# Block-sparse attention and a gated feed-forward on one core: k and q loaded in token chunks, full-width turns, scores and AV products of two pairs side by side, a split last step

## The chip, the cores and the metric

The kernel runs on one core of a Trainium2 chip. The metric is the device time of one execution in microseconds. One more execution is recorded by the hardware profiler, and all rows below come from that one. Engines are named as the profile names them: PE is TensorE's matmuls, PEld its weight loads, DVE is VectorE, ACT is ScalarE, POOL is GpSimd and SP is SyncE.

## The reference, cut to what matters

```python
batch, n_heads, seq, head_dim = 4, 8, 768, 64          # block 32, window 16
k_sum = k.reshape(B, H, nb, block, D).max(axis=3)       # 24 blocks
v_sum = v.reshape(B, H, nb, block, D).mean(axis=3)
scores_l = scale * q @ k.T            # kept where |i - j| < window
scores_s = scale * q @ k_sum.T + log(block)
a = softmax(concat([scores_l_masked, scores_s]))
x = (a @ concat([v, v_sum])).transpose(0, 2, 1, 3).reshape(3072, 512)
ffn = (gelu(x @ w_gate) * (x @ w_val)) @ w_out          # 512 -> 1536 -> 512
out = x + sigmoid(x @ w_res) * ffn
```

Inputs are float32; the matmul operands are bfloat16, and GpSimd's DMAs convert on the way in.

## The kernel before, in words

**Units.** The 3072 tokens are cut into eight units of 384, two halves of each of the four batches; unit u is half u % 2 of batch u // 2. The eight heads are four pairs hp of 128 rows (two heads of 64). The schedule is written out by hand: each engine runs its instructions in the order in which the program issues them.

**Loads and turns.** k and q come from memory with tokens on partitions. For batches 1 to 3 `load_batch` (L162) issues, on GpSimd's queue, one transfer for all of k, one for all of q (96 partitions, each with eight tokens in one run of 2 KB per head, L87), and seven for v (L96: chunks of 128 tokens with all heads, runs of 256 B). It is called within unit 0 for batch 1, and at the start of units 1 and 3 for batches 2 and 3. A turn (`turn_pair`, L169) brings one pair to d on partitions: 16 PE transposes of 96 tokens by 64 (L174), the two heads to the two halves of the partitions. ScalarE copies the result out, to `kW` (`k_step`, L178, where VectorE then adds the window's neighbours and the block maxima) or to `qT` (`q_step`, L193). In units 1, 3 and 5 each of the first eight of twelve steps `fo` turns one k or one q of the next batch.

**A unit's gate and value part.** For each of twelve `fo` there are four matmuls `g` and four `vv` (L300, 384 tokens wide), a gelu on ScalarE (L306) and a product on VectorE into `gvT` (L307). The pool `ps_mm` has four PSUM banks; `g`, `vv`, `r` and `f` take the bank that came free first.

**Block means.** `vsum_sum` (L198) takes the means of v over blocks on TensorE (`vs`, L204): seven matmuls with 32 weight columns, into partitions 96 to 127. It stands once in the start and once each in units 1, 2 and 4.

**A unit's tail.** After the twelve steps the unit's own output and the next unit's attention run in one written order (L475 to L503). For its own output there are, for each of three `sub` of 128 tokens: `r` and a tanh (`res_step`, L326), twelve `f` (`ffn_step`, L329), and `end_step` (L337: two VectorE operations `th` and `o`, and the output DMA on SyncE). For the next unit there are, for each pair: `s_step` (L234: twelve `s` matmuls of 64 rows by 64 columns, an exponential on ScalarE, a mask on VectorE giving `P`), `av_step` (L280: twelve `ao` matmuls and the normalising on VectorE, `rz` and `xn`), `xt_step` (L284: three transposes `xp` and a copy to `xT` on VectorE). There is one PSUM home each for `s` (two banks), `ao` and `xp`. So the order on TensorE is s0, r0, f0, ao0, s1, r1, four f1, ao1, s2, eight f1, ao2, s3, xp0, r2, four f2, ao3, xp1, eight f2, xp2, xp3, and then the next unit's first `g`. Unit 0 has an order of its own (L446 to L472), and in unit 7 only the output part remains.

Of the kernel before, what the change touches and what calls it, by code (L numbers as in the profile page):

```python
# [8 lines left out]
F32 = mybir.dt.float32  # L9
# [6 lines left out]
def kernel(  # L16
# [22 lines left out]
    QT = 64  # L39
# [29 lines left out]
    bmean = const.tile([128, NB - 2 + 32], BF16, name="bmean")  # L69
# [30 lines left out]
    with tc.manual_schedule():  # L100
# [42 lines left out]
        select(bmean[:], ALU.is_ge, 0.0, 32 * (NB - 2) - WIN, -32, 1)  # L143
        select(bmean[:], ALU.is_ge, 0.0, 31 + WIN - 32 * (NB - 2), 32, -1)
# [17 lines left out]
        def load_batch(b):  # L162
            k_sb[b], q_sb[b] = token_tile(0, S, "k_sb"), token_tile(0, S, "q_sb")
# [5 lines left out]
        def turn_pair(src, hp, pool, tag):  # L169
            pj = src.shape[2]  # L170
# [5 lines left out]
            return tp  # L176

        def k_step(b, hp, pool, tag):  # L178
            tp = turn_pair(k_sb[b], hp, pool, tag)
            kw = kW[b % 2][hp]  # L180
            nc.scalar.copy(kw[:, :, OWN:OWN + QT].rearrange("d t (p j) -> d t p j", j=8),  # L181
                           tp.rearrange("d j (t p) -> d t p j", t=NT))
# [10 lines left out]
        def q_step(src, b, lo, hi, hp, pool, tag):  # L193
            tp = turn_pair(src, hp, pool, tag)
            nc.scalar.copy(qT[b % 2][hp][:, lo:hi].rearrange("d (p j) -> d p j", p=PP),  # L195
                           tp.rearrange("d j p -> d p j"))

        def vsum_sum(b, pool, tag, chunks=range(NC + 1), vs=None):  # L198
            if vs is None:
                vs = pool.tile([128, DM], F32, tag=tag, name="vs")  # L200
            for c in chunks:
                lo = NB - 2 - 4 * c if c < NC else 0
                rows, t = (slice(0, 128), 2 * c) if c < NC else (slice(64, 64 + WIN), NT - 1)
                nc.tensor.matmul(vs[96:128, :], bmean[rows, lo:lo + 32], vext[b % 2][rows, t, :, 0:D],  # L204
# [29 lines left out]
        def s_step(u, hp, st, s=None):  # L234
            b, half = u // 2, u % 2
            first = s is not None
            if not first:
                s = ps_s.tile([128, 2, 512], F32, tag="s", name="s")
            kw, qt = kW[b % 2][hp], qT[b % 2][hp]
            for t in range(HT):  # L240
                tt = half * HT + t
                for hh in range(2):
                    ps = slice(hh * 64, hh * 64 + 64)
                    nc.tensor.matmul(s[:, hh, t * QT:(t + 1) * QT], kw[ps, tt, :],  # L244
# [3 lines left out]
            nc.scalar.activation(P.rearrange("p a t q -> p a (t q)"), s[:, :, 0:TU], AF.Exp,  # L248
                                 scale=scale, bias=bias_t[:])
            if not first:  # L250
                Pf = P.rearrange("p a t q -> p (a t) q")
                nc.vector.tensor_mul(Pf, Pf, maskt.unsqueeze(1).to_broadcast([128, 2 * HT, QT]))  # L252
            st["P", hp] = P

# [74 lines left out]
        def ffn_step(st, gvT, sub, lo, hi):  # L329
# [3 lines left out]
            for fo in range(lo, hi):  # L333
                nc.tensor.matmul(st["f", sub][:], gvT[:, fo, ss], w_out[:, fo, :],  # L334
                                 start=(fo == 0), stop=(fo == FO - 1))

        def end_step(u, st, sub):  # L337
            f, th = st["f", sub], st["th", sub]
            nc.vector.scalar_tensor_tensor(th[:], th[:], 1.0, f[:], ALU.add, ALU.mult)  # L339
            o = work.tile([128, DM], F32, tag="o", name="o")  # L340
            nc.vector.scalar_tensor_tensor(o[:], th[:], 0.5, st["xn"][:, sub, :], ALU.mult, ALU.add)  # L341
            row = u * TU + sub * 128
            nc.sync.dma_start(out=out[row:row + 128, :], in_=o[:])
# [72 lines left out]
        for u in range(NU):  # L416
# [29 lines left out]
            if u == 0:  # L446
# [12 lines left out]
                av_step(n, 1, nst)  # L459
# [5 lines left out]
                av_step(n, 3, nst)  # L465
# [9 lines left out]
            if nst:  # L475
                s_step(n, 0, nst)
            res_step(st, 0)
            ffn_step(st, gvT, 0, 0, FO)
            if nst:
                av_step(n, 0, nst)  # L480
                s_step(n, 1, nst)
            end_step(u, st, 0)
            res_step(st, 1)
            ffn_step(st, gvT, 1, 0, 4)
            if nst:
                av_step(n, 1, nst)
                s_step(n, 2, nst)
            ffn_step(st, gvT, 1, 4, FO)
            if nst:
                av_step(n, 2, nst)  # L490
                s_step(n, 3, nst)
                xt_step(n, 0, nst, *TT)
            end_step(u, st, 1)
            res_step(st, 2)
            ffn_step(st, gvT, 2, 0, 4)
            if nst:
# [38 lines left out]
```

## Time and profile before

| | us |
|---|---|
| runs of the kernel before | 285.95, 286.34, 287.6 |
| their median | 286.34 |
| the profiled execution's own time | 285.99 |
| its span, first to last instruction | 284.3 |
| granted TensorE clock, share of full speed | 1.00 |

The span is the part that the rows of the profile show; 1.7 us of the profiled execution's time lie around it. A row of a timeline gives the start and the duration in us, the engine, the line, the operation, the array's rows*columns for TensorE, what is written and read, and how many instructions were merged. A row of a group gives the number of instructions, then busy us and the mean ns of one, then the idle time of the engine just before them and what ended it. A row of waits gives us in total, how many, and the longest. A row of a DMA issue gives its size and the us from issue to landing. Matmuls are pipelined, so a matmul's duration overlaps the next one's.

### The profile page before, as it was taken

The page shows a single profiled execution, that of the slowest core. Times are in us where ns is not written, and L with a number is a line of the kernel's source. Part 1 is how long each engine was busy: PE and PEld are TensorE (multiplying, and loading weights), DVE is VectorE, ACT ScalarE, POOL GpSimd, SP SyncE. Part 2 cuts the span into 40 slices and gives each one's busy share as a digit, 9 for nine tenths or more (in the row PEclk, how much of TensorE's full clock was granted, in tenths as well). Part 3 has the DMA queues.
Part 4 walks back from the last instruction along what each step waited for, and adds up shares of the span by engine and source line. Part 5 has one row for each costly group of instructions (what it writes and reads, how often), then busy time and mean ns, then how long its engine had stood idle before and what let it go on. Part 6 is the DMA issues. An engine that isn't in the chain of part 4 may idle for free.

```text
span 284.3 us, 6276 instructions
## 1 busy us (share of the span) xinstructions
PE 270.6 (95%) x2607; PEld 147.5 (52%) x2632; DVE 173.2 (61%) x429; ACT 138.4 (49%) x214; POOL 44.7 (16%) x65
## 2 busy tenths in 40 slices
PE   7789997999999999999999999999999999999993
PEld 2445553555445555555555555455555555455541
DVE  3675826685557963785538855686536963683422
ACT  2855377066464335546566235446654445444310
POOL 8975532461103000040000000000000000000000
PEclk9999999999999999999999999999999999999999
DMA  6999999999952900190001100101001100101001
GB/s 89 167 179 197 201 205 208 158 241 175 171 97 55 111 0 0 39 115 19 2 0 40 76 0 1 39 37 39 2 1 39 74 2 0 39 37 39 0 37 74
DMA packets 44043, 21.36 MB, mean 75 GB/s; under 512 B 25840, under 2 KB 40944, under 8 KB 44016
## 3 DMA queue, kind: packets, MB, share of 16 engines
q0 software_dynamic: 40560, 14.68, 51.8%
q1 hardware_dynamic: 3456, 6.29, 6.0%
q8 instruction: 20, 0.33, 0.5%
q14 instruction: 7, 0.06, 0.1%
HBM read 29.36 MB, written 6.29 MB: 125 GB/s over the span
## 4 chain that ended last, share of the span: by engine, by line
PE 89%; POOL 3%; DMA 3%; issue 1%; DVE 1%; ACT 1%; POOLq 0%; DVEq 0%
PE g L300 23%; PE vv L300 22%; PE f L334 21%; PE r L318 8%; PE tp L174 4%; PE ao L268 4%; PE s L244 3%; DMA vext<-in_v_dram 3%; PE xp L287 2%; PE vs L204 2%; POOL vext L96 1%; ACT P L248 1%; PE gv L300 1%; POOL k_sb L87 1%; DVE xn L278 0%
## 5 line engine op out<-in xcount | busy, mean ns | idle before, releaser
L306 ACT ACTIVATE ge<-g 128x384 f32<-128x384 f32 x95 | 46.7, 491 | 71.0 <-DVE gvT L307 36.5
L300 PE MATMUL g<-xT,w_gate 128*128 128x384 bf16 x380 | 79.3, 327 | 0.0
L307 DVE TENSOR_TENSOR gvT<-ge,vv 128x384 bf16<-128x384 f32 x95 | 52.3, 552 | 42.9 <-PE vv L300 41.7
L300 PE MATMUL vv<-xT,w_val 128*128 128x384 bf16 x380 | 77.7, 326 | 0.0
L334 PE MATMUL f<-w_out,gvT 128*128 128x512 bf16 x274 | 65.9, 379 | 1.4 <-issue 1.1
L300 PEld LDWEIGHTS <-w_val 128*128 128x128 bf16 x384 | 37.5, 98 | 26.3 <-issue 1.9
L300 PEld LDWEIGHTS <-w_gate 128*128 128x128 bf16 x384 | 35.0, 98 | 23.5 <-issue 2.0
L248 ACT ACTIVATE P<-s,bias_t 128x768 bf16<-128x768 f32 x32 | 28.9, 902 | 28.1 <-PE s L244 28.0
L334 PEld LDWEIGHTS <-gvT 128*128 128x128 bf16 x288 | 26.9, 98 | 29.8
L96 POOL DMA_DIRECT2D vext<-in_v_dram x28 | 23.0, 830 | 63.2 <-PE ao L268 46.9
L252 DVE TENSOR_TENSOR P<-P,maskt 128x768 bf16<-128x768 bf16 x28 | 15.6, 556 | 18.0 <-ACT P L248 18.0
L318 PE MATMUL r<-w_res,xT 128*128 128x512 bf16 x88 | 24.0, 381 | 0.4
L339 DVE SCALAR_TENSOR_TENSOR th<-th,f 128x512 f32<-128x512 f32 x24 | 16.3, 681 | 8.9 <-PE f L334 8.9
L181 ACT COPY kW<-tp 128x768 bf16<-128x768 bf16 x16 | 12.8, 799 | 12.2 <-PE tp L174 12.2
L278 DVE TENSOR_TENSOR xn<-ao,rz 128x384 bf16<-128x384 f32 x32 | 17.8, 557 | 1.1
L324 ACT ACTIVATE th<-r 128x512 f32<-128x512 f32 x24 | 14.3, 594 | 8.5 <-PE r L318 8.1
L195 ACT COPY qT<-tp 128x768 bf16<-128x768 bf16 (+1 forms) x20 | 13.3, 673 | 8.9 <-PE tp L174 8.8
L341 DVE SCALAR_TENSOR_TENSOR o<-th,xn 128x512 f32<-128x512 f32 x24 | 16.6, 692 | 0.8
L268 PEld LDWEIGHTS <-P 128*64 128x64 bf16 (+2 forms) x432 | 9.5, 110 | 13.4 <-DVE P L252 5.5
L276 DVE RECIPROCAL rz<-ao 128x6 f32<-128x6 f32 x32 | 6.1, 191 | 13.6 <-PE ao L268 13.6
L268 PE MATMUL ao<-vext,P 128*64 128x65 bf16 (+1 forms) x384 | 11.8, 199 | 1.5 <-DVE xn L278 1.5
L318 PEld LDWEIGHTS <-xT 128*128 128x128 bf16 x96 | 8.1, 98 | 7.4
(66 smaller groups left out, 198.0 us busy)
## 6 DMA issues: line engine op xcount, KB each, us to landing
out_dram<-o SPq DMA_DIRECT2D x24, 256.0 KB, 2.0
vext<-in_v_dram POOLq DMA_DIRECT2D x20, 128.0 KB, 10.5
k_sb<-in_k_dram POOLq DMA_DIRECT2D x3, 768.0 KB, 11.1
q_sb<-in_q_dram POOLq DMA_DIRECT2D x3, 768.0 KB, 14.3
w_gate<-in_moe_w_gate_dram POOLq DMA_DIRECT2D x6, 256.0 KB, 8.6
w_val<-in_moe_w_val_dram POOLq DMA_DIRECT2D x6, 256.0 KB, 8.7
w_out<-in_moe_w_out_dram POOLq DMA_DIRECT2D x3, 512.0 KB, 14.1
k_sb<-in_k_dram POOLq DMA_DIRECT2D x2, 384.0 KB, 5.9
```

The source lines that it names most:

```text
L96: nc.gpsimd.dma_start(out=dst, in_=v[b, :, lo:hi, :].rearrange("h p d -> p h d"))
L248: nc.scalar.activation(P.rearrange("p a t q -> p a (t q)"), s[:, :, 0:TU], AF.Exp, scale=scale, bias=bias_t[:])
L252: nc.vector.tensor_mul(Pf, Pf, maskt.unsqueeze(1).to_broadcast([128, 2 * HT, QT]))
L268: nc.tensor.matmul(ao[64 * e:64 * e + 64, sub, hh, :], P[rows, hh, t, :], rhs, start=blocks is None or (not blocks and sub == 0 and hh == ...
L278: nc.vector.tensor_mul(xn, ao[:, :, :, 0:D], rz.to_broadcast([128, NSUB, 2, D]))
L300: nc.tensor.matmul(acc[:, 0:TU], w[:, ko, fs], st["xT"][:, ko, :], start=(ko == 0), stop=(ko == KO - 1))
L306: nc.scalar.activation(ge[:], g[:, 0:TU], AF.Gelu)
L307: nc.vector.tensor_mul(gvT[:, fo, :], ge[:], vv[:, 0:TU])
L318: nc.tensor.matmul(r[:], st["xT"][:, ko, ss], w_res[:, ko, :], start=(ko == 0), stop=(ko == KO - 1))
L334: nc.tensor.matmul(st["f", sub][:], gvT[:, fo, ss], w_out[:, fo, :], start=(fo == 0), stop=(fo == FO - 1))
L339: nc.vector.scalar_tensor_tensor(th[:], th[:], 1.0, f[:], ALU.add, ALU.mult)
L341: nc.vector.scalar_tensor_tensor(o[:], th[:], 0.5, st["xn"][:, sub, :], ALU.mult, ALU.add)
```

## The change

1. `load_batch` loads k and q of batches 1 to 3 in six chunks of 128 tokens each, with all heads in a partition's row, in runs of 256 B: 12 transfers for a batch in place of two.
2. `turn_pair` turns these by six full 128x128 transposes, one for a chunk, instead of sixteen.
3. `vsum_sum` uses 128 weight columns instead of 32, and `bmean` grows from 54 to 150 columns.
4. In the tails of units 1 to 6, s0 and s1 stand together, ao0, ao1, s2 and s3, and ao2 and ao3. s1 and s3 write two single banks, one for each head, with one exponential for each. The mask of pair 3 is issued behind `end_step` of sub 0. The `xT` copies move from VectorE to ScalarE, and each of ao and xp uses both single homes in turn.
5. In unit 0's tail ao1 and ao3 use a bank of `ps_mm`.
6. In unit 7 the last sub's `f`, `th`, `o` and output DMA are done in two halves of 256 columns.

```diff
-    bmean = const.tile([128, NB - 2 + 32], BF16, name="bmean")
+    bmean = const.tile([128, NB - 2 + 128], BF16, name="bmean")
...
-            load_tokens(k_sb[b], k, b, 0, S, 0, H)
-            load_tokens(q_sb[b], q, b, 0, S, 0, H)
+            for sb, src, name in ((k_sb, k, "k_sb"), (q_sb, q, "q_sb")):
+                sb[b] = qk.tile([128, NC, H, D], BF16, tag=name, name=name)
+                for c in range(NC):
+                    nc.gpsimd.dma_start(out=sb[b][:, c],
+                                        in_=src[b, :, c * 128:(c + 1) * 128, :].rearrange("h p d -> p h d"))
...
+            if src.shape[1] == NC:
+                tp = pool.tile([128, S], BF16, tag=tag, name="tp")
+                for c in range(NC):
+                    nc.tensor.transpose(tp[:, c * 128:(c + 1) * 128],
+                                        src[:, c, 2 * hp:2 * hp + 2, :].rearrange("p h d -> p (h d)"), ident[:])
...
-                nc.tensor.matmul(vs[96:128, :], bmean[rows, lo:lo + 32], vext[b % 2][rows, t, :, 0:D],
+                nc.tensor.matmul(vs[:], bmean[rows, lo:lo + 128], vext[b % 2][rows, t, :, 0:D],
...
-        def s_step(u, hp, st, s=None):
+        def s_step(u, hp, st, s=None, two=None, masked=True):
...
+            if two:
+                s = [pool.tile([128, 512], F32, tag=tag, name="s1") for pool, tag in two]
...
+            if two:
+                for hh in range(2):
+                    nc.scalar.activation(P[:, hh].rearrange("p t q -> p (t q)"), s[hh][:, 0:TU], AF.Exp,
+                                         scale=scale, bias=bias_t[:])
...
-                av_step(n, 1, nst)
+                av_step(n, 1, nst, *MM)
...
-                av_step(n, 3, nst)
+                av_step(n, 3, nst, *MM)
...
+                res_step(st, NSUB - 1)
+                for c0 in (0, DM // 2):
+                    ffn_step(st, gvT, NSUB - 1, 0, FO, c0, c0 + DM // 2)
+                    end_step(u, st, NSUB - 1, c0, c0 + DM // 2)
...
+            s_step(n, 0, nst)
+            s_step(n, 1, nst, two=(AO, TT))
             res_step(st, 0)
             ffn_step(st, gvT, 0, 0, FO)
...
+            res_step(st, 1)
+            av_step(n, 0, nst, *AO)
+            av_step(n, 1, nst, *TT)
+            s_step(n, 2, nst)
+            s_step(n, 3, nst, two=(MM, MM), masked=False)
             end_step(u, st, 0)
...
+            mask_part(3, nst)
+            ffn_step(st, gvT, 1, 0, 6)
+            xt_step(n, 0, nst, *AO, nc.scalar.copy)
+            ffn_step(st, gvT, 1, 6, FO)
+            xt_step(n, 1, nst, *TT, nc.scalar.copy)
+            res_step(st, 2)
+            av_step(n, 2, nst, *AO)
+            av_step(n, 3, nst, *TT)
             end_step(u, st, 1)
...
+            ffn_step(st, gvT, 2, 0, 7)
+            xt_step(n, 2, nst, *AO, nc.scalar.copy)
+            ffn_step(st, gvT, 2, 7, FO)
+            xt_step(n, 3, nst, *TT, nc.scalar.copy)
             end_step(u, st, 2)
```

How instructions stand, at three places. First TensorE's order at the beginning of unit 1's tail, where the scores and AV products of unit 2 begin; `kW_0_96` holds pair 0's keys, `vext_109` batch 1's values. Equal rows that repeat are left out. Before:

```order
L300 MATMUL vv<-xT,w_val 128x384
L244 LDWEIGHTS kW_0_96
L244 MATMUL s<-qT_0_104,kW_0_96 128x64
...
L318 LDWEIGHTS xT
L318 MATMUL r<-w_res,xT 128x512
...
L334 LDWEIGHTS gvT
L334 MATMUL f<-w_out,gvT 128x512
...
L268 LDWEIGHTS P
L268 MATMUL ao<-vext_109,P 64x65
```

Now, where `s_1731` and `s_1732` are the two single banks of pair 1:

```order
L318 MATMUL vv<-xT,w_val 128x384
L254 LDWEIGHTS kW_0_96
L254 MATMUL s<-qT_0_104,kW_0_96 128x64
...
L254 LDWEIGHTS kW_1_97
L254 MATMUL s_1731<-qT_1_105,kW_1_97 128x64
L254 MATMUL s_1732<-qT_1_105,kW_1_97 128x64
...
L336 LDWEIGHTS xT
L336 MATMUL r<-w_res,xT 128x512
...
L352 MATMUL f<-w_out,gvT 128x512
...
L336 MATMUL r<-w_res,xT 128x512
...
L286 LDWEIGHTS P
L286 MATMUL ao<-vext_109,P 64x65
```

Pair 1's scores have moved up beside pair 0's, ahead of r and f of sub 0, and r of sub 1 now stands ahead of the first ao.

Second, ScalarE's order over the tail of a unit, from the last gelus of the unit to the table load for the next. Before, of unit 3:

```order
L306 ACTIVATE ge<-g 128x384 x4
L248 ACT_TABLE_LOAD
L248 ACTIVATE P<-s,bias_t 128x768
L324 ACTIVATE th<-r 128x512
L248 ACTIVATE P<-s,bias_t 128x768
L324 ACTIVATE th<-r 128x512
L248 ACTIVATE P<-s,bias_t 128x768 x2
L324 ACTIVATE th<-r 128x512
L306 ACT_TABLE_LOAD
L306 ACTIVATE ge<-g 128x384 x6
```

Now, of the same tail:

```order
L263 ACT_TABLE_LOAD
L263 ACTIVATE P<-s,bias_t 128x768
L260 ACTIVATE P<-s_2227,bias_t 128x384
L260 ACTIVATE P<-s_2228,bias_t 128x384
L342 ACTIVATE th<-r 128x512 x2
L263 ACTIVATE P<-s,bias_t 128x768
L260 ACTIVATE P<-s_2320,bias_t 128x384
L260 ACTIVATE P<-s_2321,bias_t 128x384
L307 COPY xT<-xp 128x384 x2
L342 ACTIVATE th<-r 128x512
L307 COPY xT<-xp 128x384 x2
L324 ACT_TABLE_LOAD
```

Four copies of xT have come to ScalarE, and the table load for the next unit's gelus, which stood right behind the last tanh, stands behind the last two of them.

Third, GpSimd's loads for batch 1, from the last weights to the first of batch 2. Before:

```order
L160 DMA w_out<-in_moe_w_out_dram 128x4x512 x3
L87 DMA k_sb<-in_k_dram 96x8x512
L87 DMA q_sb<-in_q_dram 96x8x512
L96 DMA vext_109<-in_v_dram 112x8x64
L96 DMA vext_109<-in_v_dram 128x8x64 x5
L96 DMA vext_109<-in_v_dram 16x8x64
L87 DMA k_sb<-in_k_dram 96x8x512
```

Now:

```order
L160 DMA w_out<-in_moe_w_out_dram 128x4x512 x3
L166 DMA k_sb<-in_k_dram 128x8x64 x6
L166 DMA q_sb<-in_q_dram 128x8x64 x6
L96 DMA vext_109<-in_v_dram 112x8x64
L96 DMA vext_109<-in_v_dram 128x8x64 x5
L96 DMA vext_109<-in_v_dram 16x8x64
L166 DMA k_sb<-in_k_dram 128x8x64 x6
```

The order of tensors is the same; ten transfers more stand ahead of batch 1's values.

More of the change, by code (lines that the diff above doesn't have):

```diff
@@ L243, in s_step @@
                     ps = slice(hh * 64, hh * 64 + 64)
-                    nc.tensor.matmul(s[:, hh, t * QT:(t + 1) * QT], kw[ps, tt, :],
+                    nc.tensor.matmul((s[hh] if two else s[:, hh])[:, t * QT:(t + 1) * QT], kw[ps, tt, :],
                                      qt[ps, tt * QT:(tt + 1) * QT], start=not first, stop=True,
@@ L327, in res_step, with ffn_step @@
             tanh_part(st, sub, res_part(st, sub))
[L329 removed]
+        def ffn_step(st, gvT, sub, lo, hi, c0=0, c1=DM):
             ss = slice(sub * 128, (sub + 1) * 128)
```

72 lines of the change are left out of this document (28 added, 44 removed).

## The prediction

> **What bounds the kernel now.** I read the page's table of engines first, then the chain that ended last, then TensorE's timeline over one whole stage, then VectorE, ScalarE and the DMA issues for what stands behind it.
>
> ```profile
> PE 270.6 (95%) x2607; PEld 147.5 (52%) x2632; DVE 173.2 (61%) x429; ACT 138.4 (49%) x214; POOL 44.7 (16%) x65
> PE 89%; POOL 3%; DMA 3%; issue 1%; DVE 1%; ACT 1%; POOLq 0%; DVEq 0%
> ```
>
> TensorE is busy 95% of the span, and the chain runs over it for 89%. Nothing else holds the end for long, so a change pays only if TensorE's row gets shorter, or if one of its few waits goes. The next rows are TensorE's alone (start, duration, tile). Their durations overlap, so I measure from start to start.
>
> ```profile
> 72.36 1.81 PE L204 MATMUL vs<-vext,bmean 128*32 128x512 bf16 x7
> ...
> 100.06 1.81 PE L204 MATMUL vs<-vext,bmean 128*32 128x512 bf16 x7
> 101.79 0.82 PE L300 MATMUL g<-xT,w_gate 128*128 128x384 bf16 x4
> ...
> 108.30 0.81 PE L300 MATMUL g<-xT,w_gate 128*128 128x384 bf16 x4
> 108.95 0.81 PE L300 MATMUL vv<-xT,w_val 128*128 128x384 bf16 x4
> 109.70 0.35 PE L244 MATMUL s<-qT,kW 64*128 64x64 bf16 x12
> 109.98 1.04 PE L318 MATMUL r<-w_res,xT 128*128 128x512 bf16 x3
> 110.85 2.75 PE L334 MATMUL f<-w_out,gvT 128*128 128x512 bf16 x12
> 113.54 0.38 PE L268 MATMUL ao<-vext,P 128*64 128x65 bf16 x12
> 113.85 0.35 PE L244 MATMUL s<-qT,kW 64*128 64x64 bf16 x12
> 114.13 1.04 PE L318 MATMUL r<-w_res,xT 128*128 128x512 bf16 x4
> 115.01 1.03 PE L334 MATMUL f<-w_out,gvT 128*128 128x512 bf16 x4
> 115.96 0.38 PE L268 MATMUL ao<-vext,P 128*64 128x65 bf16 x12
> ...
> 123.20 0.50 PE L287 MATMUL xp<-ident,xn 128*128 128x128 bf16 x6
> 123.53 1.03 PE L300 MATMUL g<-xT,w_gate 128*128 128x384 bf16 x4
> 124.40 0.81 PE L300 MATMUL vv<-xT,w_val 128*128 128x384 bf16 x4
> 125.14 0.53 PE L174 MATMUL tp<-ident,k_sb 96*64 96x96 bf16 x16
> 125.61 0.82 PE L300 MATMUL g<-xT,w_gate 128*128 128x384 bf16 x4
> ```
>
> The reader is to see two things. There are hardly any gaps. And whatever uses only a part of the array (the shape after the operation: 64*128, 128*64, 96*64, 128*32) makes its neighbour slower. A gate chain lasts 0.65 (108.30 to 108.95). The same four matmuls take 0.75 when s follows (108.95 to 109.70), and 0.74 when a turn follows (124.40 to 125.14). Four f after a four-matmul r last 0.95 ahead of ao (115.01 to 115.96), against 0.87 for the like r (109.98 to 110.85). So to enter a partial shape costs about 0.10. The Trainium skill, TensorEngine Tiling (Array Packing), section Tiling Modes, says that changing the tiling mode drains TensorE; by that rule these tenths are drains, and the rows agree with it.
>
> **Turns of k and q.** A pair's turn is now 16 transposes of 96*64: 0.47 (125.14 to 125.61) and 0.09 on the chain ahead, 0.56 together. It becomes six full transposes of 128x128. The six xp are just that shape and take 0.33 (123.20 to 123.53), with no change of shape around them. That is 0.23 saved per turn, and there are 24 (three batches, four pairs, k and q): **5.5 us**. If an entry's tenth stayed with the new turn, 24 x 0.13 = 3.1 us would be left. A step of gate, value and turn shrinks from 1.87 to 1.63. VectorE is what is then nearest: with a k step it needs 1.76 from one product to the next.
>
> ```profile
> 60.16 0.54 DVE L307 TENSOR_TENSOR gvT<-ge,vv 128x384 bf16<-128x384 f32 x1
> 61.92 0.55 DVE L307 TENSOR_TENSOR gvT<-ge,vv 128x384 bf16<-128x384 f32 x1
> ```
>
> Only unit 1 has four k steps in a row; there VectorE falls back by 4 x 0.13 = 0.5 us, less than the step that the four banks give it, and the q steps behind have no such work. I cost it at nothing, 0.5 if that cover were gone.
>
> **Tails of units 1 to 6.** Five partial runs become three: [s0 s1], [ao0 ao1 s2 s3], [ao2 ao3]. Two entries fewer save 0.20. What runs of one kind cost side by side is seen only at the start of the kernel:
>
> ```profile
> 18.50 0.57 PE L268 MATMUL ao<-vext,P 96*64 96x65 bf16 x24
> 19.00 0.84 PE L268 MATMUL ao<-vsum,P 32*64 32x65 bf16 x24
> ```
>
> Two pairs' ao together take 0.50, so 0.25 each, where one alone takes 0.31 (113.54 to 113.85). Two adjacent places save 0.06 each. For s the trace shows no two together. Alone it takes 0.28 (109.70 to 109.98), while its columns, six times 64 at r's 512 in 0.22, are 0.16. So beside its like it saves between 0 and 0.11; I take 0.08, nearer to the ao row than to either end. Sum: 0.20 + 0.12 + 0.16 = 0.48 per unit, six units: **2.9 us**, between 1.2 (entries alone) and 3.3.
>
> That holds only if no new wait opens. From s0 to ao0 there were 3.84 us (109.70 to 113.54) and no wait; now s1 and a second r stand between as well, 3.84 + 0.20 + 0.87 = 4.9 us, against more work on ScalarE:
>
> ```profile
> L248 ACT ACTIVATE P<-s,bias_t 128x768 bf16<-128x768 f32 x32 | 28.9, 902 | 28.1 <-PE s L244 28.0
> L248 ACT ACT_TABLE_LOAD x7 | 9.0, 1283 | 0.1
> L289 ACT COPY xT<-xp 128x384 bf16<-128x384 bf16 x4 | 1.8, 480 | 1.7 <-PE xp L287 1.7
> ```
>
> One more exponential in that stretch is 0.9 us and there is 1.07 us more time, so the cover holds by little more than before, which was enough. Pairs 2 and 3 have r's 0.87 and all of f for sub 1 (2.6) between s and ao; the mask of pair 3 sits behind end_step 0 on VectorE, and it still has about 4 us. The tightest place is the unit's end. The four xT copies move to ScalarE, and the gelu table's load, which could run early, now stands behind the last of them. From the start of the last three xp: 0.33 to its end (as 0.34 in its row), 0.48 the copy, 1.28 the load, and a gelu of as many elements as the copy's, 0.48: 2.6 us. The third gate chain needs the first gelu's bank after 0.17 + 0.25 wait + 4 x 0.65 = 3.0. It is hidden by 0.4 us. The first gate chain itself already waits: 0.87 instead of 0.65 (123.53 to 124.40). Then it waits for one copy of 0.48, about 0.24. I add 0.02 x 6 = **0.1 us**.
>
> **Tail of unit 0.** ao of pairs 1 and 3 get their own bank.
>
> ```profile
> PE ao L268 <- DVE xn L278: 1.5, 3, 0.6
> ```
>
> These three waits, 1.5 us, are for the one bank. Behind them the transposes xp need the same xn from VectorE, so the wait comes back there in part, while VectorE is given its next work 0.3 to 0.7 us earlier. I take half, **0.8 us**, between 0 and 1.5.
>
> **vs.** Six of seven block-mean matmuls become full width; the last keeps 16 rows, so one entry and exit stay. Now they take 1.73 (100.06 to 101.79) and an entry of 0.10. Then there are seven at r's 0.22, an entry and an exit of 0.1 each, 1.73 in all: 0.1 x 3 = **0.3 us**, between 0 and 0.9 (no change of shape felt at all).
>
> **The split last step.**
>
> ```profile
> 277.03 2.75 PE L334 MATMUL f<-w_out,gvT 128*128 128x512 bf16 x12
> 279.89 0.69 DVE L339 SCALAR_TENSOR_TENSOR th<-th,f 128x512 f32<-128x512 f32 x1 [2.04 <-PE f L334]
> 280.61 0.69 DVE L341 SCALAR_TENSOR_TENSOR o<-th,xn 128x512 f32<-128x512 f32 x1
> ```
> ```profile
> L278 DVE TENSOR_TENSOR xn<-ao,rz 128x384 bf16<-128x384 f32 x32 | 17.8, 557 | 1.1
> ```
>
> From 384 to 512 columns VectorE grows by 0.13 (0.56 to 0.69), so 256 columns take about 0.42. After the last matmul 0.42 + 0.42 stand instead of 0.69 + 0.69: 0.5 us; the last output DMA is half as big (one more on SyncE's queue, nothing behind it), 0 to 0.2. **0.6 us.** The same columns pass TensorE, and twice the weight loads hide as they do under the 128-column xp.
>
> **Start.** bmean is nearly three times as wide, and its two selects stand ahead of five of GpSimd's loads of v:
>
> ```profile
> 6.95 0.54 POOL L115 TENSOR_SCALAR_AFFINE_SELECT bmean<-bmean 128x54 bf16<-128x54 bf16 x2
> ```
>
> By width alone 0.54 becomes 1.5; part is fixed, and the loads behind queue at the DMA. I add **0.1 us**, between 0 and 1.0.
>
> **Loads.** k and q of batches 1 to 3 are 36 chunks of the shape of v's, in place of six big transfers, on GpSimd's queue. They are hidden now; these rows say how well (issue, then us to landing):
>
> ```profile
> 30.97 0.79 POOL L87 DMA_DIRECT2D k_sb<-in_k_dram  x1 [0.51 <-DMA w_val<-in_moe_w_val_dram]
> 32.30 0.77 POOL L87 DMA_DIRECT2D q_sb<-in_q_dram  x1 [0.54 <-DMA w_gate<-in_moe_w_gate_dram]
> 45.83 0.87 POOL L96 DMA_DIRECT2D vext<-in_v_dram  x1 [1.67 <-DMA w_out<-in_moe_w_out_dram]
> ```
> ```profile
> k_sb<-in_k_dram POOLq DMA_DIRECT2D x1, 768.0 KB, 18.4
> ```
> ```profile
> q_sb<-in_q_dram POOLq DMA_DIRECT2D x1, 768.0 KB, 21.0
> ```
> ```profile
> vext<-in_v_dram POOLq DMA_DIRECT2D x1, 128.0 KB, 13.3
> ```
>
> k lands at 49.4, q at 53.3, the sixth chunk of v at 59.1. So 768 KB took 3.9 in long rows and 5.8 in six chunks, 0.97 a chunk, and k's transfer began near 45.5. At 0.97 a chunk k lands at 51.3, q at 57.1, v at 63.0. The vs of that batch stands at 72.36, less 0.8 and eight turns' 1.8: 69.7; the first turn, eight steps of 1.87 ahead of the old 72.36 and 0.8 earlier, at 56.6. All is hidden, k by 5 us, v by 6.7, and I cost it at nothing; if the cover went, the price is rival 1. The Trainium skill, DMA: Bandwidth & Descriptors, section Specifications, asks for 512 B or more per transfer for line rate, which speaks against pieces of 256 B; the row agrees (5.8 against 3.9).
>
> **Sum.** 5.5 + 2.9 + 0.8 + 0.3 + 0.6 - 0.1 - 0.1 = 9.9 us off the profiled execution's 285.99 gives 276.1. The median of the three runs lies 0.35 higher, so I say **276.4**.
>
> **Rivals.** (1) *The chunks come late, and it ends slower.* At c us a chunk v of batch 1 lands at 45.5 + 18c and is late from c = 1.34; v of batch 2, 36 chunks on, is needed at its vs, 100.06 less some 3.3, so 96.8, and is late from c = 1.43. It eats all 9.9 us at c = (106.7 - 45.5)/36 = 1.70; at c = 1.8 it lands at 110.3, a wait of 13.5, and the time is 276.4 + 13.5 = 290. For it: smaller pieces, and a GpSimd issue of 0.87 for each. Against it: 0.97 measured for the same shape in the same queue. (2) *A wait in the tail takes the gain's place*, at the late table load: if the second gate chain rather than the third wants the first gelu's bank, 1.3 us sooner, the 0.4 of cover turns into a wait of 0.9, six times 5.4: 281.8. For it: the thin cover. Against it: the sums above. (3) *The change of shape was not the cost*: turns save 3.1, tails 1.2 and vs nothing, 5.5 with the rest: 280.8. For it: no trace of before has two s together. Against it: the xp rows. (4) *A full transpose does not overlap with the next*, and each costs its whole duration:
>
> ```profile
> L287 PE MATMUL xp<-ident,xn 128*128 128x128 bf16 x96 | 9.6, 220 | 0.1
> ```
>
> A turn would then be 6 x 0.22 = 1.32 instead of 0.56, 18.2 us more for 24, and with 4.4 off by the other terms 300.1. Against it: six xp follow each other at 0.055, and only a difference between xp and k's turn could let it in. The Trainium skill, TensorE: Matmul & The Clock Gate, section Part 4: PE-mode transpose, speaks for it with about 275 ns per 128x128 transpose in one kernel; by that a turn would be 1.65 us, and the trace does not bear it out.
>
> **How the numbers follow.** Forecast 0.80, rival 1 0.05, rival 2 0.08, rival 3 0.06, rival 4 0.01. The bounds of the terms give 5.6 + 3.3 + 1.5 + 0.9 + 0.8 = 12.1 at best, 274.2, and rival 3 bounds the worse side with some of rival 2: I say 274.0 to 281.0. About 0.5% is what a measurement of this kernel can tell from no change. Forecast, rivals 2 and 3 are all faster, 0.94; rival 1 is same in 0.02 and slower in 0.03, rival 4 slower in 0.01.
>
> **What would show it.** In the changed kernel's TensorE timeline a turn should take 0.33 to 0.36 and the vv ahead of it 0.65; [s0 s1] near 0.5, [ao0 ao1 s2 s3] near 1.0; g after the last xp 0.85 to 0.9; in unit 0 waits on xp of under 0.8 in sum; 0.42 for th and o at the end; no wait of TensorE for a load after the start. A wait of TensorE for k_sb, q_sb or vext, a wait of the third g of a unit for a gelu, or turns that still take 0.45 would make me wrong.

## The result, and the profile after

| | before | after |
|---|---|---|
| times, us | 285.95, 286.34, 287.6, 289.1 | 275.1, 277.39, 277.68, 277.88 |
| median, us | 286.97 | 277.53 |
| the profiled execution's own time | 285.99 | 277.88 |
| its span | 284.3 | 276.2 |
| its granted TensorE clock | 1.00 | 0.986 |

After takes 0.9644 of the time of before (95% interval 0.9563 to 0.9724). The forecast was 276.4, with 274.0 to 281.0 as its range: faster, at nearly the forecast size. But the 1.1 us that the median lies above it are the difference of two larger errors of opposite sign, and the traces let us name both.

Here are the page's table of engines, the first line of the chain that ended last, and the granted clock in 40 slices of the span, all of after:

```profile
PE 263.9 (96%) x2379; PEld 150.6 (55%) x2404; DVE 169.5 (61%) x407; ACT 147.6 (53%) x250; POOL 71.8 (26%) x95
PE 86%; POOL 3%; DMA 3%; DVE 3%; ACT 2%; issue 2%; POOLq 0%; DVEq 0%
PEclk9986999999999999999999999999999999999999
```

TensorE is still the bound, at 96% of a shorter span. GpSimd's busy time grew from 44.7 to 71.8, which are the many small loads, and the end did not feel it. What is new is the dip in the clock in the third and the fourth slice, some 14 to 28 us after the start (a slice is 6.9 us).

Next comes TensorE's timeline of after, from the end of unit 1's steps through the tail into unit 2 (start, duration, tile; I measure from start to start):

```profile
108.35 0.81 PE L318 MATMUL vv<-xT,w_val 128*128 128x384 bf16 x4
109.09 0.52 PE L254 MATMUL s<-qT,kW 64*128 64x64 bf16 x24
109.55 1.04 PE L336 MATMUL r<-w_res,xT 128*128 128x512 bf16 x3
...
113.01 1.03 PE L336 MATMUL r<-w_res,xT 128*128 128x512 bf16 x4
113.97 0.57 PE L286 MATMUL ao<-vext,P 128*64 128x65 bf16 x24
114.47 0.52 PE L254 MATMUL s<-qT,kW 64*128 64x64 bf16 x24
114.93 1.47 PE L352 MATMUL f<-w_out,gvT 128*128 128x512 bf16 x5
...
122.10 0.33 PE L305 MATMUL xp<-ident,xn 128*128 128x128 bf16 x3
122.26 1.05 PE L318 MATMUL g<-xT,w_gate 128*128 128x384 bf16 x4
123.16 0.81 PE L318 MATMUL vv<-xT,w_val 128*128 128x384 bf16 x4
123.80 0.50 PE L176 MATMUL tp<-ident,k_sb 128*128 128x128 bf16 x6
124.14 0.81 PE L318 MATMUL g<-xT,w_gate 128*128 128x384 bf16 x4
```

A turn takes 0.34 (123.80 to 124.14) and the chain ahead of it 0.64, where before it was 0.47 and 0.74. The pair of scores takes 0.46 (109.09 to 109.55), the pair of AV products 0.50 (113.97 to 114.47). The first gate chain waits, 0.90 instead of 0.65 (122.26 to 123.16).

Put together from such starts, the span divides like this. "Steps" are the twelve gate and value steps with the turns and block means that stand among them; "tail" goes from the first s to the next unit's first g.

| stretch | before | after | difference |
|---|---|---|---|
| start, to unit 0's first s | 39.70 | 42.62 | +2.92 |
| unit 0's tail | 16.33 | 15.51 | -0.82 |
| steps of unit 1 (eight turns, vs) | 22.08 | 20.11 | -1.97 |
| steps of units 3 and 5 (eight turns each) | 40.90 | 37.23 | -3.67 |
| steps of units 2 and 4 (vs) | 35.51 | 35.35 | -0.16 |
| steps of units 6 and 7 (neither) | 31.73 | 31.78 | +0.05 |
| tails of units 1 to 6 | 83.01 | 79.03 | -3.98 |
| unit 7's output, to the end | 15.04 | 14.57 | -0.47 |
| span | 284.3 | 276.2 | -8.1 |

Without the first row the change gains 11.0 us. With it, 8.1 are left in this execution. The first row goes with the clock. This is a view by stretches, us 8 to 28, first of before and then of after (the stretch and its length; the busy time of PE, PEld, DVE, ACT and POOL; the granted clock, the DMA's share and its GB/s):

```profile
8.00:28.00 20.00, 16.83 (x273) 9.99 (x271) 12.51 (x36) 12.81 (x22) 14.71 (x20) 1.00 1.95 180
```
```profile
8.00:28.00 20.00, 16.95 (x260) 10.19 (x256) 10.43 (x31) 11.24 (x20) 14.90 (x20) 0.83 1.83 181
```

And TensorE's timeline of after within it:

```profile
16.74 0.38 PE L212 MATMUL vs<-vext,bmean 128*128 128x512 bf16 x1 [0.43 <-DMA vext<-in_v_dram]
17.65 0.70 PE L212 MATMUL vs<-vext,bmean 128*128 128x512 bf16 x2 [0.53 <-DMA vext<-in_v_dram]
...
24.79 0.53 PE L318 MATMUL gv<-xT,w_gate 128*128 128x384 bf16 x1
25.11 0.53 PE L318 MATMUL gv<-xT,w_val 128*128 128x384 bf16 x1
...
26.43 0.33 PE L318 MATMUL gv<-xT,w_val 128*128 128x384 bf16 x1
26.59 0.33 PE L318 MATMUL g<-xT,w_gate 128*128 128x384 bf16 x1
```

Matmuls of 384 columns follow each other at 0.32 (24.79 to 25.11) and a microsecond later at 0.16 (26.43 to 26.59): for a few us the array ran at half rate, and then no more. Whether the change did this is a question for the experiments. One of the four executions of after had a clock of 1.00, and it is the one of 275.1.

At the end, VectorE and TensorE of after:

```profile
269.40 2.78 PE L352 MATMUL f<-w_out,gvT 128*128 128x256 bf16 x24
...
272.22 0.42 DVE L357 SCALAR_TENSOR_TENSOR th<-th,f 128x256 f32<-128x256 f32 x1 [0.36 <-PE f L352]
272.67 0.42 DVE L359 SCALAR_TENSOR_TENSOR o<-th,xn 128x256 f32<-128x256 f32 x1
```

From the first f to the end of o it takes 3.69 (269.40 to 273.09); before it took 4.27 (277.03 to 281.30). The halved operations take the forecast 0.42 each. The last output transfer brought nothing: from o's end to the end of the span it is 3.1, against 3.0.

### The profile page after: what moved, and what is told of

The parts are those of the page before. It is cut to its first block, busy times and chain, and to the rows that moved or that the text cites. A ratio compares the mean times of both kernels' runs of the same rounds, so it can differ in the third digit from the quotient of the medians.

```text
span 276.2 us, 5877 instructions
## 1 busy us (share of the span) xinstructions
PE 263.9 (96%) x2379; PEld 150.6 (55%) x2404; DVE 169.5 (61%) x407; ACT 147.6 (53%) x250; POOL 71.8 (26%) x95
## 4 chain that ended last, share of the span: by engine, by line
PE 86%; POOL 3%; DMA 3%; DVE 3%; ACT 2%; issue 2%; POOLq 0%; DVEq 0%
PE f L352 22%; PE vv L318 22%; PE g L318 21%; PE r L336 8%; PE ao L286 3%; PE tp L176 3%; DMA vext<-in_v_dram 3%; PE s L254 2%; PE xp L305 2%; PE vs L212 2%; POOL vext L96 2%; ACT xT L307 1%; PE gv L318 1%; ACT P L263 1%; DVE gvT L325 1%
## 5 line engine op out<-in xcount | busy, mean ns | idle before, releaser
L352 PE MATMUL f<-w_out,gvT 128*128 128x512 bf16 (+1 forms) x286 | 68.0, 371 | 0.8 <-issue 0.2
L318 PEld LDWEIGHTS <-w_gate 128*128 128x128 bf16 x384 | 36.2, 98 | 21.4 <-issue 1.2
L307 ACT COPY xT<-xp 128x384 bf16<-128x384 bf16 x28 | 13.3, 478 | 25.1 <-PE xp L305 25.1
L342 ACT ACTIVATE th<-r 128x512 f32<-128x512 f32 x24 | 14.4, 598 | 17.4 <-PE r L336 17.4
L357 DVE SCALAR_TENSOR_TENSOR th<-th,f 128x512 f32<-128x512 f32 (+1 forms) x25 | 16.6, 662 | 9.8 <-PE f L352 9.8
L263 ACT ACTIVATE P<-s,bias_t 128x768 bf16<-128x768 f32 x20 | 18.1, 904 | 3.5 <-PE s L254 3.4
L166 POOL DMA_DIRECT2D k_sb<-in_k_dram x18 | 15.9, 894 | 6.7 <-DMA w_out<-in_moe_w_out_dram 1.7
L359 DVE SCALAR_TENSOR_TENSOR o<-th,xn 128x512 f32<-128x512 f32 (+1 forms) x25 | 16.8, 670 | 0.9
L166 POOL DMA_DIRECT2D q_sb<-in_q_dram x18 | 15.7, 885 | 5.6 <-DMA w_out<-in_moe_w_out_dram 3.4
```

The source lines that it names most:

```text
L166: nc.gpsimd.dma_start(out=sb[b][:, c], in_=src[b, :, c * 128:(c + 1) * 128, :].rearrange("h p d -> p h d"))
L307: copy(st["xT"][:, ko, :], xp[:])
L318: nc.tensor.matmul(acc[:, 0:TU], w[:, ko, fs], st["xT"][:, ko, :], start=(ko == 0), stop=(ko == KO - 1))
L352: nc.tensor.matmul(st["f", sub][:, 0:c1 - c0], gvT[:, fo, ss], w_out[:, fo, c0:c1], start=(fo == 0), stop=(fo == FO - 1))
L357: nc.vector.scalar_tensor_tensor(th, th, 1.0, f[:, 0:c1 - c0], ALU.add, ALU.mult)
L359: nc.vector.scalar_tensor_tensor(o[:, 0:c1 - c0], th, 0.5, st["xn"][:, sub, c0:c1], ALU.mult, ALU.add)
```

## Experiments

The forecast rests on one theory, called A in the expectations: TensorE's row is the time, and what a partial shape costs goes when the shape goes. The other letters are the rivals that each expectation names. The granted clock differs from one execution to the next, so beside the medians I compare executions of like clock, and stretches of the traces, which it hardly touches after the start.

**Turns and loads alone.** The kernel before, with the chunked loads and the full transposes and nothing else of the change.

```diff
-            load_tokens(k_sb[b], k, b, 0, S, 0, H)
-            load_tokens(q_sb[b], q, b, 0, S, 0, H)
+            for sb, src, name in ((k_sb, k, "k_sb"), (q_sb, q, "q_sb")):
+                sb[b] = qk.tile([128, NC, H, D], BF16, tag=name, name=name)
+                for c in range(NC):
+                    nc.gpsimd.dma_start(out=sb[b][:, c],
+                                        in_=src[b, :, c * 128:(c + 1) * 128, :].rearrange("h p d -> p h d"))
...
+            if src.shape[1] == NC:
+                tp = pool.tile([128, S], BF16, tag=tag, name="tp")
+                for c in range(NC):
+                    nc.tensor.transpose(tp[:, c * 128:(c + 1) * 128],
+                                        src[:, c, 2 * hp:2 * hp + 2, :].rearrange("p h d -> p (h d)"), ident[:])
```

> The kernel before with the chunked loads and the full 128x128 turns of k and q alone. Theory A (what a turn cost beside its columns was the change of the array's shape): a step of gate, value and turn goes from 1.87 to 1.64, 24 x 0.23 = 5.5 us less. Rival B (the change of shape was not the cost, an entry's tenth stays): 3.1 us less. If the start's lower clock comes from the loads or the turns, it shows here; if it comes from another part, the granted clock is 1.00 as in the profile of before.

Measured: 282.96 (280.4 to 283.69), a ratio of 0.9824 (0.975 to 0.9898). At a clock of 0.998 it took 280.4, where executions of before at 1.00 took 285.6 to 286.4, so some 5.5 less. The stretches say it without the clock: the steps of units 1, 3 and 5 take 20.22, 18.59 and 18.59, together 5.58 less than before, or 0.23 a turn; the other stretches after the start are those of before. A holds. The start took 3.3 us longer in the profiled execution, at a granted clock of 0.984, although this kernel has neither the wider block means nor the new tails.

**Half-width turns.** The changed kernel, with each transpose as two of 64 columns of the array: the loads, the data and everything else as in after.

```diff
-                    nc.tensor.transpose(tp[:, c * 128:(c + 1) * 128],
-                                        src[:, c, 2 * hp:2 * hp + 2, :].rearrange("p h d -> p (h d)"), ident[:])
+                    for hh in range(2):
+                        nc.tensor.transpose(tp[hh * 64:hh * 64 + 64, c * 128:(c + 1) * 128],
+                                            src[:, c, 2 * hp + hh, :], ident[:])
```

> The changed kernel, but each 128x128 transpose is made as two of 64 columns side by side: the same loads, the same columns streamed, 12 instructions instead of 6, in a partial shape (128*64). Theory A: a turn costs about 0.55 again with the tenth on the vv ahead of it, 24 x 0.2 = 4.8 to 5.5 us more than the changed kernel. Rival C (it was the number of instructions, 16 against 6): with 12 a turn costs some 0.14 more than the full one by proportion, 3.3 us more, and vv ahead of it stays 0.65.

Measured: 283.48 (281.11 to 283.64), a ratio of 0.9839 (0.9771 to 0.9907); 6 us above after. TensorE's timeline at the same place as above:

```profile
125.28 0.81 PE L319 MATMUL vv<-xT,w_val 128*128 128x384 bf16 x4
126.02 0.53 PE L177 MATMUL tp<-ident,k_sb 128*64 128x128 bf16 x12
126.48 0.82 PE L319 MATMUL g<-xT,w_gate 128*128 128x384 bf16 x4
```

Twelve half-width transposes take 0.46, nearly what the old sixteen took, and the chain ahead of them is at 0.74 again. A step is 0.23 longer than after's; over 24 turns that is 5.5, and the steps of units 1, 3 and 5 are indeed 5.45 longer. Using half the array's columns for the same data brings back all that the turns had gained, where the larger number of instructions by itself was expected to cost 3.3. Of the 0.23 a turn, 0.10 stands on the chain ahead, where rival C expected nothing. The other 0.12 lies within the turn, near the 0.14 that rival C expected there. The number of instructions does not explain it, for before's sixteen took 0.47, hardly more than these twelve. But the expectation is wrong that the same columns are streamed: by the rows, the identity's columns that pass are 12 times 128 here, as many as the 16 times 96 of before, and 6 times 128 in after. Whether the 0.12 belongs to them or to the shape was not tried apart. The Trainium skill, TensorEngine Tiling (Array Packing), section Tiling Modes, says that a change of tiling mode drains TensorE. The 0.10 on the neighbouring chain agrees with that; its size is known here from these rows alone.

**Tails alone.** The kernel before, with the new tails of units 1 to 6 (the order, the banks, the exponentials and the copies on ScalarE, item 4 of the change) and nothing else.

```diff
+            s_step(n, 0, nst)
+            s_step(n, 1, nst, two=(AO, TT))
...
-                av_step(n, 0, nst)
-                s_step(n, 1, nst)
+            av_step(n, 0, nst, *AO)
+            av_step(n, 1, nst, *TT)
+            s_step(n, 2, nst)
+            s_step(n, 3, nst, two=(MM, MM), masked=False)
```

> The kernel before, with the new order of the tails of units 1 to 6 alone (scores and AV products of two pairs side by side); turns, loads, vs, unit 0 and the last step as before. The trace of the changed kernel has 0.63 us less per tail (14.70 before, 14.07 now), so 6 x 0.63 = 3.8 less than before. By the term on record (0.46 per unit with the longer wait of g) it would be 2.8 less. A third reading, that the tails gain only beside the faster turns, would give nothing. At equal granted clock: 282.1 against 283.1 against 285.9.

Measured: 283.67 (282.02 to 285.12), a ratio of 0.9906 (0.9864 to 0.9948). The profiled execution had a clock of 1.00 and took 282.02, 4.0 less than before's 285.99. Its tail, on TensorE:

```profile
108.94 0.52 PE L246 MATMUL s<-qT,kW 64*128 64x64 bf16 x24
...
122.11 1.05 PE L310 MATMUL g<-xT,w_gate 128*128 128x384 bf16 x4
```

13.17 where before takes 13.83, in every one of the six. The term on record, 2.9, was too small; 3.8 to 4.0 is right, and it needs nothing of the turns.

**The small edits alone.** The kernel before, with the wide block means, the other bank for two AV products in unit 0, and the split last step.

```diff
-    bmean = const.tile([128, NB - 2 + 32], BF16, name="bmean")
+    bmean = const.tile([128, NB - 2 + 128], BF16, name="bmean")
...
-                av_step(n, 1, nst)
+                av_step(n, 1, nst, *MM)
...
+                for c0 in (0, DM // 2):
+                    ffn_step(st, gvT, NSUB - 1, 0, FO, c0, c0 + DM // 2)
+                    end_step(u, st, NSUB - 1, c0, c0 + DM // 2)
```

> The kernel before, with the small edits alone: bmean and vs over 128 rows, the other bank for two AV steps of unit 0, and the split last step. The terms on record are 0.3 + 0.8 + 0.6 = 1.7 less, less 0.1 for the wider selects. The traces agree with each (vs 3 x 0.1, unit 0's tail 0.82, the end 0.58), so 284.3 at the clock at which before takes 285.9. If part of the 0.82 of unit 0 belongs to the chunked loads or the turns, it is 285 or more.

Measured: 285.55 (284.59 to 287.53), a ratio of 0.9982 (0.9939 to 1.0026): as a whole time not told apart from before. Here the clock hides the term. In the trace unit 0's tail is 15.51 (before 16.33), the three stretches with block means are 0.10 shorter each, and the part from unit 7's first r to the end is 14.5 (before 15.04): 1.6 to 1.7 less, as forecast. The start took 1.5 more in that execution. At a clock of 0.998 the kernel took 284.59, some 1.3 less than before at 1.00.

**Two more warm matmuls in the start.** The changed kernel, with two scratch matmuls each behind the fourth and the fifth block-mean matmul of the start, where TensorE waits for v.

```diff
-        vsum_sum(0, *MM, range(3, NC + 1), vs)
+        for lo, hi in ((3, 4), (4, 5), (5, NC + 1)):
+            vsum_sum(0, *MM, range(lo, hi), vs)
+            if hi <= NC:
+                keep_warm(2)
```

> The changed kernel with two warm matmuls behind the fourth and the fifth block-mean matmul of the start, where TensorE waited 0.43 and 0.53 us for v. Theory D (the changed start leaves TensorE idle enough for the granted clock to fall at 19 to 26 us, which costs 2.5 us): the clock is 1.00 in every run and the time 275.1 as in the one run of the changed kernel at 1.00. Rival E (the fall comes by chance, whatever these gaps are): clocks of 0.986 still appear, and the median stays near 277.5.

Measured: 275.33 (274.98 to 275.82), a ratio of 0.9576 (0.952 to 0.9632). The four executions had clocks of 0.991 or 1.00, none of 0.986, and the times are those that theory D expected; only its 1.00 in every run did not come. The profiled one had a shorter dip at another place, from about 12.5 to 16 us, ahead of the added matmuls: unit 0's first s stands at 40.28, 0.6 behind before's and 2.3 ahead of after's.

**Before, unchanged, again.**

> The kernel before, unchanged, for the granted clock of each of its runs. Theory D: 1.00 in all, so that the changed start is what brought the lower clock. Rival E: 0.986 in some, about 288.5 us there against 286 in the others.

Measured: 285.61 to 288.99 over ten executions. They fall by their clock: 285.61 to 285.92 at 0.999 to 1.00, 286.62 to 287.69 at 0.99, 288.84 to 288.99 at 0.986 to 0.987. So the kernel before has the same fall and pays the same 3 us for it. The profiled execution, of 288.9, shows where. This is its clock in 40 slices, and then its first s of unit 0:

```profile
PEclk9996999999999999999999999999999999999999
```
```profile
42.61 0.35 PE L244 MATMUL s<-qT,kW 64*128 64x64 bf16 x12
```

That s stands at 42.61 in the unchanged kernel too, where after has it at 42.62 and before's first profile at 39.70, and the spans differ by the same 2.9 (287.2 against 284.3). Of the executions whose clock is on record, 11 of 40 of before had 0.998 or more, and 3 of 10 of after. That the change brings the fall about is refuted; that it makes it somewhat more or less frequent, these counts cannot tell.

**Small chunks.** The changed kernel, with k and q in chunks of 32 tokens: 48 transfers for a batch in place of 12, the same bytes in the same 256-byte runs.

```diff
-                    nc.gpsimd.dma_start(out=sb[b][:, c],
-                                        in_=src[b, :, c * 128:(c + 1) * 128, :].rearrange("h p d -> p h d"))
+                    for e in range(0, 128, 32):
+                        nc.gpsimd.dma_start(out=sb[b][e:e + 32, c],
+                                            in_=src[b, :, c * 128 + e:c * 128 + e + 32, :].rearrange("h p d -> p h d"))
```

> The changed kernel, with k and q of batches 1 to 3 in chunks of 32 tokens instead of 128: four times as many transfers (48 a tensor pair and batch more than half as long in GpSimd's issue), the same 256-byte rows and the same sum of bytes. It tests the price at which the loads come late. By the theory that the issue sets the pace of this queue, one issue each of about 0.6 to 0.9 us as in the trace: 128 tokens take 2.4 us or more, v of batch 1 lands 6 us or more after TensorE wants it, and TensorE waits for vext: 6 to 15 us slower than the changed kernel, 284 to 293. By the theory that the rows' own transfer (0.97 per 128 tokens) sets the pace, no wait: 277.5, the same as the changed kernel.

Measured: 294.88 (294.47 to 295.16), a ratio of 1.0298 (1.0275 to 1.0321): slower than before, by the mechanism of the first rival, and 17.4 above after, more than was expected. GpSimd's timeline of this kernel:

```profile
56.15 7.38 POOL L167 DMA_DIRECT2D q_sb<-in_q_dram  x13
63.89 2.28 POOL L167 DMA_DIRECT2D q_sb<-in_q_dram  x4 [0.35 <-DMA q_sb<-in_q_dram]
66.80 3.98 POOL L167 DMA_DIRECT2D q_sb<-in_q_dram  x7 [0.63 <-issue]
70.76 5.74 POOL L96 DMA_DIRECT2D vext<-in_v_dram  x7
```

The issue paces it: 0.57 each (7.38 over 13), so four of them, 128 tokens, take 2.3 where the one issue takes 0.87. v of batch 1 is issued from 70.76 instead of 50.74. TensorE of the same kernel shows what that costs:

```profile
67.58 0.22 PE L177 MATMUL tp<-ident,q_sb 128*128 128x128 bf16 x1 [0.83 <-DMA q_sb<-in_q_dram]
70.44 0.22 PE L177 MATMUL tp<-ident,q_sb 128*128 128x128 bf16 x1 [2.64 <-DMA q_sb<-in_q_dram]
73.12 0.26 PE L177 MATMUL tp<-ident,q_sb 128*128 128x128 bf16 x1 [2.47 <-DMA q_sb<-in_q_dram]
73.18 1.48 PE L319 MATMUL g<-xT,w_gate 128*128 128x384 bf16 x4
74.46 1.48 PE L319 MATMUL vv<-xT,w_val 128*128 128x384 bf16 x4
```

The first thing to come late is q, not v as I had written: q's first turn, which reads every chunk of q, stands ahead of v's first use (65.97 and 72.51 in after). And the wait costs more than its length: after 5.9 us of waits the next gate chain takes 1.28 (73.18 to 74.46) instead of 0.65. The steps of unit 1 are 9.0 longer than after's and those of unit 2, where TensorE waits 3.7 for v, 7.0; the 6 to 15 expected had no fall of the clock in it.

**A late gelu.** The changed kernel, with two scratch copies on ScalarE ahead of the load of the gelu table at each unit's end.

```diff
             xt_step(n, 3, nst, *TT, nc.scalar.copy)
+            for _ in range(2):
+                nc.scalar.copy(warm[:, 0:TU], nst["xT"][:, 2, :])
```

> The changed kernel, with two scratch copies of 0.48 us on ScalarE between the last xT copy and the load of the gelu table, at the end of units 0 to 5's tails' own order (units 1 to 6), which delays the first gelu by 0.96 us. In the trace of the changed kernel the first gelu ends 0.40 us before the third gate chain starts in the four units that have no turns there (93.86 and 94.26) and 1.03 in the two that have (124.74 and 125.77). If the third chain is the one that wants the gelu's bank, four units wait (0.96 - 0.40) = 0.56 each and two none: 2.2 us slower than the changed kernel, 279.7. If the second chain wanted it, the wait would be there already, and the copies would add 0.96 x 6 = 5.8: 283.3. If the gelu has more room than the rows say, no change: 277.5.

Measured: 280.89 (279.64 to 281.26), a ratio of 0.9803 (0.9774 to 0.9832). Its waits of TensorE, the line for gelu, and then TensorE's timeline where unit 2's gate chains begin, one of the four places without turns:

```profile
PE g L318 <- ACT ge L324: 1.9, 4, 0.5
```
```profile
93.74 0.81 PE L318 MATMUL g<-xT,w_gate 128*128 128x384 bf16 x4
94.39 0.81 PE L318 MATMUL vv<-xT,w_val 128*128 128x384 bf16 x4
95.69 0.81 PE L318 MATMUL g<-xT,w_gate 128*128 128x384 bf16 x4 [0.49 <-ACT ge L324]
```

It is the third gate chain that waits, four times, and only where no turn stands among the steps. The stretches of those four units are 0.65, 0.65, 0.64 and 0.65 longer than after's, together 2.6, the two with turns not at all. (The other 0.8 of this profiled execution are the start's.) The copies moved the gelu by 0.97 against the first gate chain, so the cover in after is 0.97 - 0.65 = 0.32 us. The forecast said 0.4.

**Both kernels beaten.** The warm matmuls, and the last xT step of each tail two f matmuls sooner (behind f 9 instead of f 11; the expectation calls it three), to remove the wait of the first gate chain. The diff shows the second edit; the first is that of the warm matmuls above. The unchanged after ran in the same rounds.

```diff
-            ffn_step(st, gvT, 2, 7, FO)
+            ffn_step(st, gvT, 2, 7, 10)
             xt_step(n, 3, nst, *TT, nc.scalar.copy)
+            ffn_step(st, gvT, 2, 10, FO)
```

> The changed kernel with two edits: the four warm matmuls of the start (as in warm_start) and the last xT step of each unit's tail moved three f chains sooner in sub 2 (behind f 7 to 9 instead of behind f 7 to 11), so that its copy is done before the next unit's first gate chain. In the trace of the changed kernel that chain takes 0.90 instead of 0.65 in each of the six tails; if the wait for the copy is the cause, 6 x 0.24 = 1.4 us less than warm_start's 275.3: 273.9. If the same time comes back as a wait of xp for sub 2's xn or of f for the next bank, nothing: 275.3. The window of 0.31 to 0.40 us ahead of the gelu grows by the same move, so no wait there in either case.

> The changed kernel unchanged, in the same rounds as the version with the two edits, for a comparison on one chip. By the runs so far 277.5 (275.1 to 277.9), its time going with the granted clock of the start.

Measured: 273.77 (273.29 to 274.54), a ratio of 0.9519 (0.9472 to 0.9565); after in the same rounds 276.98 (275.1 to 278.45), 0.9614 (0.9553 to 0.9675). TensorE at the end of unit 1's tail in the new version:

```profile
118.44 0.33 PE L305 MATMUL xp<-ident,xn 128*128 128x128 bf16 x3
118.61 0.59 PE L352 MATMUL f<-w_out,gvT 128*128 128x512 bf16 x2
119.04 0.81 PE L318 MATMUL g<-xT,w_gate 128*128 128x384 bf16 x4
119.69 0.81 PE L318 MATMUL vv<-xT,w_val 128*128 128x384 bf16 x4
```

The first gate chain takes 0.65 (119.04 to 119.69) instead of 0.90, in all six places: 1.44 less in the sum of the stretches, as expected. The clock of the start is 1.00, and unit 0's first s stands at 39.63.

## Why the prediction was right, and where it was not

**Turns: right.** 5.5 on record; 0.23 a turn in after's rows, 5.58 alone, 5.45 back again with half the width.

**Tails: mechanism right, size too small.** 2.9 on record, with 0.1 to be added for g. The new stretch from the first s to the next g is 0.66 shorter in each of six, less 0.02 to 0.03 that g's longer wait takes back: 3.8. The step that failed is "Two adjacent places save 0.06 each". The row behind it was right: two pairs' AV products take 0.50 together in the tail too. But 0.25 against 0.31 is a saving for each of the two in a place, so a place saves 0.62 - 0.50 = 0.12, and I counted it once. For s I took 0.08 a place, and it is 0.10 (twice 0.28, less 0.46). With these the sum is 0.20 + 0.24 + 0.20 = 0.64 a tail, against the measured 0.66.

**Unit 0, block means, last step: right.** 0.82 (on record 0.8), 0.1 for each of three (0.3), and 0.58 from f to o (0.5 of the 0.6). The 0.1 for the smaller transfer did not come. In unit 0 transposes wait, as forecast, but for less, and only one of the two waits is for `xn`; the other is for the copy `xT`:

```profile
49.66 0.34 PE L305 MATMUL xp<-ident,xn 128*128 128x128 bf16 x3 [0.31 <-DVE xn L296]
51.59 0.33 PE L305 MATMUL xp<-ident,xn 128*128 128x128 bf16 x3 [0.31 <-DVE xT L307]
```

0.62 of waits where 1.5 stood before; the tail as a whole is 0.82 shorter.

**Loads: right.** No wait of TensorE for k_sb, q_sb or vext after the start. This is the issue of v of batch 1 in GpSimd's timeline of after, and then the group of those transfers among the DMA issues, with the us from issue to landing:

```profile
50.74 5.22 POOL L96 DMA_DIRECT2D vext<-in_v_dram  x6
```
```profile
vext<-in_v_dram POOLq DMA_DIRECT2D x5, 128.0 KB, 7.1
```

0.87 an issue, the last of the six at 55.1, landing at about 62.2; I had worked out 63.0. The first rival needed 1.34 a chunk. The small chunks, at 2.3, show that its mechanism is real; a pace nearer to 1.34 was not tried.

**Second rival: not it, but near.** After has no wait of a gate chain for a gelu. With the late gelu it is the third chain that waits, as the forecast's sum had it, and not the second; the cover was 0.32. A delay of 0.97 us there costs 2.6 in all.

**Start: wrong.** I put 0.1 there, for the wider selects. They take 0.70 instead of 0.54 together and no one waits for them: in the last version, with the warm matmuls and a clock of 1.00, unit 0's first s stands 0.07 earlier than in before. What was missing is that the profiled execution of before was a lucky one. It had a clock of 1.00; 29 of 40 executions of before were under 0.998. One profile cannot show that, and the forecast's offset of 0.35, from profile to median, rested on three runs. In after's profiled execution the fall costs 2.5 us up to the first full gate chain (27.64 against 25.13), and 0.4 more behind it, where TensorE waits for one product on VectorE. That last 0.4 appears in no trace whose clock stayed at 1.00; why the later start brings it wasn't tried.

At equal clock the account closes: 5.5 + 3.8 + 0.8 + 0.3 + 0.5 = 10.9, and 285.99 - 275.1 = 10.9. The forecast's 9.9 was 1.0 too little, nearly all of it the tails' term. The median is 2.4 above that execution, with the clock of the start, and only 0.35 of that was in the forecast. The two errors have opposite signs, and 1.1 is left. So the turns, unit 0, the block means and the last step were right term by term, but that the whole came so near was partly luck. Where more executions were set against each other the gain is nearer to the account: 287.71 and 276.98, 10.7 apart, in the last experiment.

## What to carry to other kernels

Where TensorE bounds, price a partial shape on both sides: here about 0.10 us on the chain ahead, and as much again once in each run, whether it held one pair or two (scores take 0.28 alone and 0.46 for two); so put runs of one kind side by side, or make them full width. Before costing an edit against one profiled execution, look at that execution's granted clock: a stretch of the trace that is compared start to start shows a term of 0.1 us where whole times differ by 3. When a load is cut into pieces, the issue's time for each piece, not the bytes, can become its pace, and it is late at the first piece that someone waits for.

## What was not expected of the hardware

TensorE's clock falls to half in short stretches without any long wait. In after's start the longest waits of TensorE between 12 and 20 us are 0.53, 0.43 and 0.40, and from about 19 to 26 us its matmuls follow each other at half rate. With four more matmuls of 512 columns there, none of ten executions had a clock under 0.991; without them six of ten of after had 0.984 to 0.988. The Trainium skill, TensorE: Matmul & The Clock Gate, section Part 1: The HAM clock gate, tells of a free-running window of about 3.4 us and of a fall to half rate after an idle window. The half rate agrees (0.32 against 0.16), and a free-running window would explain that the same program falls in one execution and not in the next. But no stretch of 3.4 us ahead of the fall was idle here, so the fall came without what the page asks for. No run here shows the window itself.

A wait of TensorE can cost more than its length. With the small chunks 5.9 us of waits for q were followed by some 5 us at half rate:

```profile
66.00:80.00 14.00, 8.06 (x44) 4.53 (x43) 3.19 (x9) 3.83 (x8) 13.30 (x21) 0.76 1.38 87
```

The granted clock is 0.76 over this stretch (66 to 80 us), and the steps of that unit grew by 9.0 us, 3.1 more than the waits.

GpSimd's issue time is mostly fixed: 0.57 us for 32 KB, 0.87 for 128 KB, in runs of 256 B both times.
